# First expert layer with the high and low parts of its moving operand in one matmul, three arms of widths, and part of the weights' low parts on GpSimd

## The chip, the cores and the metric

The kernel runs on one core of one Trainium2 chip. The metric is the device time of one execution in microseconds (us). The engines are TensorE (PE in the rows, PEld for its weight loads), VectorE (DVE), ScalarE (ACT), GpSimd (POOL) and SyncE (SP, which issues most DMAs).

## What is computed

Three layers in a row, all in fp32: a sparse attention (8 global keys and a local window of 96), a mixture of 8 experts in which each token goes to one expert, and a second mixture in which each token goes through 4 experts, weighted.

```python
idx = np.argmax(logits, axis=1)                 # one of 8 experts for each of 1536 tokens
for e in range(8):                              # D = 512, F = 1024
    h = np.maximum(x[idx == e] @ w1[e], 0.0)
    out[idx == e] = gate_w[idx == e, None] * (h @ w2[e])
...
for e in range(4):
    h = np.maximum(x @ v1[e], 0.0)
    out += p[:, e:e + 1] * (h @ v2[e])
```

The change is in the first mixture, the loop over 8 experts. The router of the reference, worked out on its inputs, gives the experts 171, 247, 155, 177, 135, 215, 231 and 205 tokens.

## The kernel before, in words

fp32 products are made out of fp32r matmuls: every operand is cut into a high part (a copy rounded to fp32r) and a low part (operand minus high part), and a product is the sum of three matmuls, high x high, low x high and high x low.

**The loop of the first mixture** has 64 stages, `st = 8 * e + i`. Each uses one quarter of a weight matrix, a [128, 1024] block (512 KB). Stages 0 to 3 of an expert make the hidden layer (lines 892 to 894): two blocks f of 128 hidden units, each a sum over c = 0..3 of three matmuls, with 128 weight columns loaded for each matmul and the expert's token columns moving. Stages 4 to 7 make the output (907 to 909) in four PSUM tiles `yp[d]`, in the same way. So an expert takes 8 stages of 24 matmuls. The tokens of an expert stand in 256 columns; `each_width` branches on TensorE at run time (line 833, one branch in each stage) between 256 and 232 moving columns, by a flag that `offsets` computes from the counts. Expert 0 always takes 256 columns.

**Behind the matmuls.** `relu3` makes the hidden layer's high part on ScalarE (line 779) and its low part on VectorE (780), both out of PSUM. `flip_x` transposes the next expert's tokens on TensorE (857, four transposes) in stages 4 and 5 and cuts them with `split3` (775, 776). At the end of an expert `split3` cuts the four `yp[d]` into `x2h` and `x2l`, the input of the second mixture, at a column offset that is read at run time. The three hidden tiles rotate in the PSUM pool `ps_h`.

**The weights** run ahead. SyncE loads a block into one of 4 `raw` buffers (line 85). `split_to(st + 7)` puts the high part of block st + 6 on ScalarE (123), behind the `relu3` of stage st, and one stage later `split_low` puts its low part on VectorE (93). The load of block i + 5 is issued when the low part of block i is done. High and low parts lie in a ring of 14 tiles, seven blocks.

**Each engine works through its own queue in the order in which the program is written** (`manual_schedule`); across engines it waits on semaphores. The order within a stage is the order of the source.

**Around it.** `records` writes 12 indirect DMAs from GpSimd (821) after stage 20. In the last expert, after stages 61 and 62, GpSimd and ScalarE begin the second mixture's weights: `w_t13` (170, 171), `w_op` (ScalarE 181, GpSimd 182) and `w_t24` (174, 175). Then the last `split3` follows, and the second mixture starts with the matmuls of line 1023 (on `x2h`) and 1024 (on `x2l`), d by d. In the second mixture GpSimd makes low parts of weight blocks of [128, 1024] too (line 162).

## Time and profile before

| what | value |
|---|---|
| median of 3 runs | 794.27 us (794.21 to 795.54) |
| the profiled execution | 795.5 us, of which the span of the profile is 793.6 us |
| TensorE busy | 780.2 us (98% of the span), weight loads 717.6 us |
| VectorE, ScalarE, GpSimd busy | 537.7, 355.0 and 262.2 us |
| granted TensorE clock, mean over the span | 0.996 of full speed |

The span runs from the first to the last recorded instruction of the execution; 1.9 us of the execution lie outside it. Matmuls are pipelined and their ends are modelled, so that a matmul's own duration is longer than the distance to the next one; what a matmul costs in a stream is read from the starts.

### The profile page before, as it was taken

Reading aid. Unit: us, or ns where it says so; the run is one execution under the profiler, and the core shown is the slowest. Engines: PE = TensorE matmul, PEld = TensorE weight load, DVE = VectorE, ACT = ScalarE, POOL = GpSimd, SP = SyncE. Lnnn points to the kernel's source line nnn. Section 1 sums busy time; section 2 is a strip of 40 time slices with the busy share of each in tenths; the row PEclk is TensorE's granted clock in tenths of the full one; section 3 lists DMA queues with packets and bytes.
Section 4 is the critical chain, followed back from the end, with each engine's and each line's share of the span. In section 5 each row is a group of like instructions: output and inputs, shape, how many; then the busy total and the mean of one; then the engine's idle time right before and its main releaser. Section 6 shows DMA issues by size and latency. Waiting matters only on the chain.

```text
span 793.6 us, 14813 instructions
## 1 busy us (share of the span) xinstructions
PE 780.2 (98%) x5706; PEld 717.6 (90%) x5706; DVE 537.7 (68%) x1305; ACT 355.0 (45%) x728; POOL 262.2 (33%) x240
## 2 busy tenths in 40 slices
PE   9999999999999999999999999999999999999995
PEld 5889899999999989999899999999899999989995
DVE  7888675866666546556766766766777766676674
ACT  7899476755555544442242232332233233223221
POOL 2026560260000431451361351362163145136222
PEclk9999999999999999999999999999999999999998
DMA  7986375666665410010000100010001001000111
GB/s 223 327 287 221 119 232 201 217 210 231 217 221 201 149 54 27 28 53 27 28 27 27 54 27 27 27 54 27 27 27 55 28 27 54 1 1 1 54 54 57
DMA packets 32314, 77.97 MB, mean 98 GB/s; under 512 B 3865, under 2 KB 10281, under 8 KB 32225
## 3 DMA queue, kind: packets, MB, share of 16 engines
q1 hardware_dynamic: 29792, 70.36, 26.6%
q0 software_dynamic: 2416, 6.39, 2.3%
q8 instruction: 58, 0.95, 0.5%
q14 instruction: 32, 0.25, 0.1%
q10 hardware_dynamic: 16, 0.02, 0.0%
HBM read 66.22 MB, written 10.53 MB: 97 GB/s over the span
## 4 chain that ended last, share of the span: by engine, by line
PE 84%; DVE 8%; ACT 3%; DMA 1%; issue 1%; POOL 1%; POOLq 0%; SPq 0%; DVEq 0%; ACTq 0%
PE h L1024 10%; PE h L1023 10%; PE h L1025 10%; PE z L1117 9%; PE z L1120 9%; PE z L1119 9%; PE h L892 4%; PE h L893 4%; PE h L894 4%; PE y L909 4%; PE y L907 4%; PE y L908 4%; DVE sh L1074 2%; PE s L501 2%; PE at L528 1%; PE o L542 1%
## 5 line engine op out<-in xcount | busy, mean ns | idle before, releaser
L993 DVE SCALAR_TENSOR_TENSOR xall<-z,rsb,xall 128x256 f32<-128x256 f32 x313 | 135.2, 478 | 35.2 <-PE z L1120 34.6
L1024 PE MATMUL h<-x2l,wh 128*128 128x512 f32 (+1 forms) x400 | 152.8, 382 | 0.0
L1023 PE MATMUL h<-x2h,wh 128*128 128x512 f32 (+1 forms) x400 | 152.8, 382 | 0.0
L1025 PE MATMUL h<-x2h,wl 128*128 128x512 f32 (+1 forms) x400 | 152.2, 381 | 0.0
L1117 PE MATMUL z<-wt,sh 128*128 128x256 f32 x384 | 109.4, 285 | 0.8 <-ACT sh L1082 0.3
L1120 PE MATMUL z<-wt,sl 128*128 128x256 f32 x384 | 108.9, 284 | 0.0
L1119 PE MATMUL z<-wt,sh 128*128 128x256 f32 x384 | 108.6, 283 | 0.0
L1045 POOL TENSOR_TENSOR bl<-h,bh 128x512 fp32r<-128x512 f32 (+1 forms) x25 | 31.9, 1275 | 189.0 <-PE z L1120 164.5
L1060 ACT ACTIVATE ah<-h 128x512 fp32r<-128x512 f32 (+1 forms) x50 | 29.1, 582 | 140.6 <-PE h L1025 140.6
L1025 PEld LDWEIGHTS h<-x2h,wl 128*128 128x128 f32 x400 | 75.3, 188 | 14.7
L1023 PEld LDWEIGHTS h<-x2h,wh 128*128 128x128 f32 x400 | 75.4, 188 | 13.2
L1024 PEld LDWEIGHTS h<-x2l,wh 128*128 128x128 f32 x400 | 75.4, 188 | 12.9 <-issue 0.2
L1117 PEld LDWEIGHTS z<-wt,sh 128*128 128x128 f32 x384 | 73.5, 191 | 3.2 <-DVE xall L993 1.8
L1033 ACT ACTIVATE h<-h 128x512 f32<-128x512 f32 (+1 forms) x50 | 28.7, 573 | 103.4 <-PE h L1025 103.4
L93 DVE TENSOR_TENSOR wl<-raw,wh 128x1024 fp32r<-128x1024 f32 x62 | 74.5, 1222 | 0.0
L1119 PEld LDWEIGHTS z<-wt,sh 128*128 128x128 f32 x384 | 73.6, 192 | 0.8
L1120 PEld LDWEIGHTS z<-wt,sl 128*128 128x128 f32 x384 | 73.5, 192 | 0.3 <-DVE sl L1083 0.3
L907 PE MATMUL y<-hh,wh 128*128 128x232 f32 (+1 forms) x256 | 71.8, 280 | 0.0
L909 PE MATMUL y<-hh,wl 128*128 128x232 f32 (+1 forms) x256 | 70.6, 276 | 0.0
L908 PE MATMUL y<-hl,wh 128*128 128x232 f32 (+1 forms) x256 | 70.6, 276 | 0.0
L182 POOL TENSOR_TENSOR wt<-raw,wt 128x512 fp32r<-128x512 f32 x40 | 51.5, 1299 | 57.6 <-ACT wt L181 50.4
L1039 DVE SCALAR_TENSOR_TENSOR ss<-h,h 128x256 f32<-128x256 f32 (+1 forms) x50 | 20.5, 410 | 68.9 <-ACT h L1033 68.9
(210 smaller groups left out, 1999.6 us busy)
## 6 DMA issues: line engine op xcount, KB each, us to landing
raw<-in_moe_w_dram SPq DMA_DIRECT2D x96, 512.0 KB
xs<-zt SPq DMA_DIRECT2D x4, 1024.0 KB
xr<-xs SPq DMA_DIRECT2D x14, 256.0 KB
v<-in_v_dram SPq DMA_DIRECT2D x12, 256.0 KB
k<-in_k_dram SPq DMA_DIRECT2D x11, 256.0 KB
q<-in_q_dram SPq DMA_DIRECT2D x11, 256.0 KB
vwin<-in_v_dram SPq DMA_DIRECT2D x10, 192.0 KB
xe<-xs SPq DMA_DIRECT2D x2, 256.0 KB
```

Source lines behind the costliest of these rows:

```text
L93: eng.tensor_tensor(lo, r, hi.bitcast(F32), ALU.subtract)
L182: nc.gpsimd.tensor_tensor(t[:, 1], src, t[:, 0].bitcast(F32), ALU.subtract)
L907: nc.tensor.matmul(y_, wh[:, f, ws], a_, start=kf == 0, stop=False, skip_group_check=True)
L908: nc.tensor.matmul(y_, wh[:, f, ws], b_, start=False, stop=False, skip_group_check=True)
L909: nc.tensor.matmul(y_, wl[:, f, ws], a_, start=False, stop=kf == KF - 1, skip_group_check=True)
L993: nc.vector.scalar_tensor_tensor(a_, src[:, i], w_, a_, ALU.mult, ALU.add)
L1023: nc.tensor.matmul(pt, wh[:, d, ws], x2h[:, d, cs], start=d == 0, stop=False)
L1024: nc.tensor.matmul(pt, wh[:, d, ws], x2l[:, d, cs], start=False, stop=False)
L1025: nc.tensor.matmul(pt, wl[:, d, ws], x2h[:, d, cs], start=False, stop=d == KD - 1)
L1117: nc.tensor.matmul(pt[:, i], hh[:, f, ts_], wh[:, f, :], start=(o_ < 3 or pt is not prods[o_][3]) and i == f == 0, stop=False, skip_group_ ...
L1119: nc.tensor.matmul(pt[:, i], hh[:, f, ts_], wl[:, f, :], start=False, stop=False, skip_group_check=True)
L1120: nc.tensor.matmul(pt[:, i], hl[:, f, ts_], wh[:, f, :], start=False, stop=f == 1, skip_group_check=True)
```

## The change

Four things. The moving operand's high and low parts lie side by side (`xhl`, `hhl`, `x0`), and one matmul of twice the width multiplies both by the weights' high part into two halves of one PSUM tile; a second matmul adds the weights' low part times the operand's high part to the first half. So there are two matmuls where there were three, over the same number of columns. Whoever reads such a tile has to add the halves: `h_sum` does it on VectorE for the hidden layer (into `hs` in SBUF, one reduction for each f), `h_high` and `h_low` then work from `hs`, and `y_low` does it for the output, in two VectorE instructions for each half of d, moved to stages 0 and 1 of the next expert. PSUM holds four tiles of one f each (`hp`, which `flip_x` and `offsets` now use too) and `yp` in four banks. There are three arms, 184, 232 and 256 columns, and the branch is taken for each f. From stage 8 on the weights' low parts are made on GpSimd in the first 6 stages of an expert (experts 1 to 4) or the first 4 (experts 5 to 7), and on VectorE in the others. The 12 indirect DMAs of `records` move to stages 42 to 53, one in each, and the clearing of `x2l` by two stages.

```diff
-WIDTHS = 232, 256
+WIDTHS = 184, 232, 256
...
-    def split_to(n):
+    def split_to(n, eng=nc.vector):
-        split_low()
+        split_low(eng)
...
-        xh0, xl0 = (ring.tile([P, 1024], F32R, tag="w", name="x0").rearrange("p (k n) -> p k n", k=KD) for _ in range(2))
+        x0 = [ring.tile([P, 1024], F32R, tag="w", name="x0").rearrange("p (k a n) -> p k a n", k=2, a=2) for _ in range(2)]
         for c in range(KD):
-            nc.scalar.copy(xh0[:, c, :], xy[c])
-            nc.vector.tensor_tensor(xl0[:, c, :], xy[c], xh0[:, c, :].bitcast(F32), ALU.subtract)
+            xc = x0[c // 2][:, c % 2]
+            nc.scalar.copy(xc[:, 0, :], xy[c])
+            nc.vector.tensor_tensor(xc[:, 1, :], xy[c], xc[:, 0, :].bitcast(F32), ALU.subtract)
...
-        ps_h = mo.enter_context(tc.tile_pool(name="ps_h", bufs=3, space=PSUM))
...
-        def relu3(pt, hi, lo):
-            nc.scalar.activation(hi, pt, AF.Relu)
-            nc.vector.scalar_tensor_tensor(lo, pt, 0.0, hi.bitcast(F32), ALU.max, ALU.subtract)
...
+            ps_1 = m1.enter_context(tc.tile_pool(name="ps_1", bufs=1, space=PSUM))
...
-                pt = ps_t.tile([P, NE], F32, tag="t", name="t")
+                pt = next(hp)[:, 0, 0:NE]
...
+                nc.vector.scalar_tensor_tensor(arm, cnt[:, 0:NE], float(WIDTHS[1]), over, ALU.is_gt, ALU.add)
...
                 for t_ in range(T):
                     nc.gpsimd.indirect_dma_start(recv[t_], bass.IndirectOffsetOnAxis(ap=ri[:, t_:t_ + 1].bitcast(U32), axis=0),
                                                  rsrc[:, t_, :], None, bounds_check=NT - 1, oob_is_err=False)
+                    yield
...
                     with tc.If(wide > 0) as over:
-                        yield WIDTHS[1]
+                        with tc.If(wide > 1) as full:
+                            yield WIDTHS[2]
+                        with full.Else():
+                            yield WIDTHS[1]
                     with over.Else():
                         yield WIDTHS[0]
...
-            xh = mp1.tile([P, KD, CAP], F32R, name="xh")
-            xl = mp1.tile([P, KD, CAP], F32R, name="xl")
-            hh = mp1.tile([P, KF, CAP], F32R, name="hh")
-            hl = mp1.tile([P, KF, CAP], F32R, name="hl")
+            xhl = mp1.tile([P, KD, 2, CAP], F32R, name="xhl")
+            hhl = mp1.tile([P, KF, 2, CAP], F32R, name="hhl")
+            hs = mp1.tile([P, 2, 2, CAP], F32, name="hs")
+            late = []
 
             def flip_x(e, s_):
-                if e == 0 and s_:
-                    pt = next(hp).rearrange("p f (a n) -> p (f a) n", n=P)
-                else:
-                    pt = ps_t.tile([P, KD, P], F32, tag="t", name="t")
+                pt = next(hp).rearrange("p a (b n) -> p (a b) n", n=P)
                 x_ = xr.pop((e, s_))
                 for c in range(KD):
                     nc.tensor.transpose(pt[:, c, :], x_[:, c * P:(c + 1) * P], ident)
-                split3(pt, xh[:, :, s_ * P:(s_ + 1) * P], xl[:, :, s_ * P:(s_ + 1) * P])
+                split3(pt, xhl[:, :, 0, s_ * P:(s_ + 1) * P], xhl[:, :, 1, s_ * P:(s_ + 1) * P])
+
+            def h_sum(pt, f):
+                nc.vector.tensor_reduce(hs[:, f // 2 % 2, f % 2, :], pt.rearrange("p a n -> p n a"), AX.X, ALU.add)
+
+            def h_high(i):
+                nc.scalar.activation(hhl[:, 2 * i:2 * i + 2, 0, :], hs[:, i % 2], AF.Relu)
+                late.append(i)
+
+            def h_low():
+                while late:
+                    i = late.pop(0)
+                    hi, lo = (hhl[:, 2 * i:2 * i + 2, a] for a in range(2))
+                    nc.vector.scalar_tensor_tensor(lo, hs[:, i % 2], 0.0, hi.bitcast(F32), ALU.max, ALU.subtract)
+
+            ends = []
+
+            def y_low(j):
+                if ends:
+                    d, o_ = ends.pop(0)
+                    hi, lo = (a[:, d:d + 2, bass.ds(o_, CAP)] for a in (x2h, x2l))
+                    nc.vector.tensor_tensor(hs[:, j], yp[:, d:d + 2, 0, :], hi.bitcast(F32), ALU.subtract)
+                    nc.vector.tensor_tensor(lo, yp[:, d:d + 2, 1, :], hs[:, j], ALU.add)
+
+            def low_on(st):
+                return nc.gpsimd if st >= 8 and st % 8 < (6 if st < 40 else 4) else nc.vector
...
+                if st == 4:
                     nc.gpsimd.memset(x2l.bitcast(F32), 0.0)
                 if 2 <= st < 2 + T:
                     square(mp1, st - 2)
                 if st == 3 or 2 + T <= st:
                     next(parts, None)
                 if st == 8 + T:
-                    records(sorted_[1])
+                    sorted_[3] = records(sorted_[1])
+                if st >= 42:
+                    next(sorted_[3], None)
...
-            hp = cycle([ps_h.tile([P, 2, CAP], F32, tag="h", name="h") for _ in range(3)])
-            yp = [ps_y.tile([P, CAP], F32, tag=f"y{d}", name="y") for d in range(KD)]
+            hp = cycle([ps_1.tile([P, 2, CAP], F32, tag=f"h{j}", name="h") for j in range(4)])
+            yp = ps_y.tile([P, KD, 2, CAP], F32, name="y")
             wide = None
             for e in range(NE):
-                xa, xb = (xh, xl) if e else (xh0, xl0)
                 for i in range(4):
                     st = 8 * e + i
                     wh, wl = use(st)
-                    pt = next(hp)
-                    for w_ in each_width(e, wide):
-                        for f in range(2):
-                            ws = slice(f * P, (f + 1) * P)
+                    for f in range(2):
+                        pt = next(hp)
+                        ws = slice(f * P, (f + 1) * P)
+                        for w_ in each_width(e, wide):
                             for c in range(KD):
-                                o_, a_, b_ = pt[:, f, 0:w_], xa[:, c, 0:w_], xb[:, c, 0:w_]
-                                nc.tensor.matmul(o_, wh[:, c, ws], a_, start=c == 0, stop=False)
-                                nc.tensor.matmul(o_, wh[:, c, ws], b_, start=False, stop=False)
-                                nc.tensor.matmul(o_, wl[:, c, ws], a_, start=False, stop=c == KD - 1)
-                    relu3(pt, hh[:, 2 * i:2 * i + 2, :], hl[:, 2 * i:2 * i + 2, :])
-                    split_to(min(st + PRE, W0 + 2))
+                                a_ = (xhl[:, c] if e else x0[c // 2][:, c % 2])[:, :, 0:w_]
+                                nc.tensor.matmul(pt[:, :, 0:w_], wh[:, c, ws], a_, start=c == 0, stop=False)
+                                nc.tensor.matmul(pt[:, 0, 0:w_], wl[:, c, ws], a_[:, 0], start=False, stop=c == KD - 1)
+                        h_sum(pt, 2 * i + f)
+                    h_low()
+                    h_high(i)
+                    if i < 2:
+                        y_low(1 - i)
+                    split_to(min(st + PRE, W0 + 2), low_on(st))
                     side(st)
                 for i in range(4):
                     st = 8 * e + 4 + i
                     wh, wl = use(st)
-                    for w_ in each_width(e, wide):
-                        for f in range(2):
-                            kf = 2 * i + f
+                    for f in range(2):
+                        kf = 2 * i + f
+                        for w_ in each_width(e, wide):
                             for d in range(KD):
                                 ws = slice(d * P, (d + 1) * P)
-                                y_, a_, b_ = yp[d][:, 0:w_], hh[:, kf, 0:w_], hl[:, kf, 0:w_]
-                                nc.tensor.matmul(y_, wh[:, f, ws], a_, start=kf == 0, stop=False, skip_group_check=True)
-                                nc.tensor.matmul(y_, wh[:, f, ws], b_, start=False, stop=False, skip_group_check=True)
-                                nc.tensor.matmul(y_, wl[:, f, ws], a_, start=False, stop=kf == KF - 1, skip_group_check=True)
+                                a_ = hhl[:, kf, :, 0:w_]
+                                nc.tensor.matmul(yp[:, d, :, 0:w_], wh[:, f, ws], a_, start=kf == 0, stop=False, skip_group_check=True)
+                                nc.tensor.matmul(yp[:, d, 0, 0:w_], wl[:, f, ws], a_[:, 0], start=False, stop=kf == KF - 1, skip_group_check=True)
+                    h_low()
                     if e + 1 < NE and i < 2:
                         flip_x(e + 1, i)
                     if e + 1 < NE and i == 2:
                         ahead = wider(e + 1)
                     if i == 2 and e + 2 < NE:
                         load_x(e + 2)
-                    split_to(min(st + PRE, W0 + 2))
+                    split_to(min(st + PRE, W0 + 2), low_on(st))
                     side(st)
...
+                for d in range(0, KD, 2):
+                    nc.scalar.copy(x2h[:, d:d + 2, bass.ds(o_, CAP)], yp[:, d:d + 2, 0, :])
+                    ends.append((d, o_))
+                if e == NE - 1:
+                    for j in range(2):
+                        y_low(j)
...
-                for d in range(KD):
-                    split3(yp[d], x2h[:, d, bass.ds(o_, CAP)], x2l[:, d, bass.ds(o_, CAP)])
...
+            ps_h = m2.enter_context(tc.tile_pool(name="ps_h", bufs=3, space=PSUM))
```

## Rows read from the trace of the kernel before

**Rows 1.** The page: GB/s moved by DMA, in 40 equal slices of the span.

```profile
GB/s 223 327 287 221 119 232 201 217 210 231 217 221 201 149 54 27 28 53 27 28 27 27 54 27 27 27 54 27 27 27 55 28 27 54 1 1 1 54 54 57
```

**Rows 2.** Windows: start:end, length, busy time (and instructions) of PE, PEclk, DMA share, GB/s.

```profile
111.01:134.67 23.66, 23.66 (x203) 1.00 0.60 205
...
157.48:179.79 22.31, 22.31 (x203) 1.00 0.66 209
```

**Rows 3.** Windows, one expert: length, busy PE, PEld, DVE, ACT, POOL, PEclk, DMA.

```profile
188.20:210.50 22.30, 22.30 (x202) 22.30 (x202) 15.00 (x20) 13.59 (x22) 0.00 (x0) 1.00 0.62 213
```

**Rows 4.** Timeline of PE: start us, length us, engine, line, out<-in, shape, count.

```profile
143.62 0.27 PE L892 MATMUL h<-xh,wh 128*128 128x232 f32 x1
...
146.29 0.28 PE L892 MATMUL h<-xh,wh 128*128 128x232 f32 x1
...
280.03 0.39 PE L1025 MATMUL h<-x2h,wl 128*128 128x512 f32 x1
...
282.75 0.39 PE L1025 MATMUL h<-x2h,wl 128*128 128x512 f32 x1
```

**Rows 5.** Groups by form, 90 to 275 us: matmuls of line 892 by width.

```profile
L892 PE MATMUL h<-xh,wh 128*128 128x232 f32 x192 | 52.6, 274 | 0.0
...
L892 PE MATMUL h<-xh,wh 128*128 128x256 f32 x32 | 9.0, 281 | 0.0
```

**Rows 6.** Groups by form: count | busy us, mean ns | idle before.

```profile
L93 DVE TENSOR_TENSOR wl<-raw,wh 128x1024 fp32r<-128x1024 f32 x62 | 74.5, 1222 | 0.0
...
L530 DVE COPY ats<-at 128x512 f32<-128x512 f32 x10 | 6.9, 690 | 2.2 <-PE at L528 2.2
...
L287 DVE TENSOR_REDUCE l<-lh 128x8 f32<-128x64 f32 x12 | 3.2, 264 | 0.0
...
L288 DVE TENSOR_REDUCE sm<-l 128x1 f32<-128x8 f32 x12 | 1.9, 161 | 0.4
...
L814 DVE TENSOR_REDUCE r__1868<-tmp 128x12 f32<-128x96 f32 x1 | 0.3, 253 | 0.0
...
L821 POOL DMA_INDIRECT rec<-rsrc,ri x12 | 16.2, 1354 | 41.7 <-DVE hl L780 38.4 <-issue 3.4
```

**Rows 7.** Timeline of DVE: starts that follow each other without a wait.

```profile
173.07 0.69 DVE L780 SCALAR_TENSOR_TENSOR hl<-h,hh 128x512 fp32r<-128x512 f32 x1 [1.81 <-issue]
173.67 1.22 DVE L93 TENSOR_TENSOR wl<-raw,wh 128x1024 fp32r<-128x1024 f32 x1
174.81 0.68 DVE L780 SCALAR_TENSOR_TENSOR hl<-h,hh 128x512 fp32r<-128x512 f32 x1
```

**Rows 8.** Timeline of DVE and POOL, second mixture.

```profile
386.18 2.41 POOL L162 TENSOR_TENSOR wl<-raw,wh 128x1024 fp32r<-128x1024 f32 x1
...
387.20 1.94 DVE L1050 TENSOR_TENSOR sl<-ss,sh 128x512 fp32r<-128x512 f32 x1
388.55 1.75 POOL L170 TENSOR_TENSOR t<-raw 128x512 f32<-128x512 f32 x1
...
390.38 1.29 POOL L171 TENSOR_TENSOR raw<-raw 128x512 f32<-128x512 f32 x1
```

**Rows 9.** One line's durations, ns min/median/max.

```profile
L1062 DVE SCALAR_TENSOR_TENSOR al<-h,ah x50: 413/681/683, 286.2 to 779.6; 128x512 fp32r<-128x512 f32 x46, 128x256 fp32r<-128x256 f32 x4
```

**Rows 10.** Timeline of the passage to the second mixture, POOL, ACT and PE.

```profile
269.59 1.58 POOL L171 TENSOR_TENSOR raw<-raw 128x512 f32<-128x512 f32 x1 [1.79 <-ACT wt L181]
...
274.94 1.16 ACT L181 ACTIVATE wt<-raw 128x512 fp32r<-128x512 f32 x2 [3.11 <-POOL raw L174]
...
276.00 1.22 ACT L775 CAST x2h<-y 128x256 f32 x4
...
276.59 0.41 PE L1023 MATMUL h<-x2h,wh 128*128 128x512 f32 x1
...
276.96 0.47 PE L1024 MATMUL h<-x2l,wh 128*128 128x512 f32 x1
```

**Rows 11.** One line's durations, ns min/median/max: TensorE's branches.

```profile
L833 PEldq COMPARE_BRANCH  x64: 65/208/342, 117.8 to 271.9; - x64
```

More of the change, by code (lines that the diff above doesn't have):

```diff
@@ L784, in tile_attention_moe_moe @@
             xp = m1.enter_context(tc.tile_pool(name="xp", bufs=4))
+            ps_1 = m1.enter_context(tc.tile_pool(name="ps_1", bufs=1, space=PSUM))
             ps_y = m1.enter_context(tc.tile_pool(name="ps_y", bufs=1, space=PSUM))
             nc.gpsimd.memset(x2h.bitcast(F32), 0.0)
-            ps_t = m1.enter_context(tc.tile_pool(name="ps_t", bufs=1, space=PSUM))
             rsrc = mp1.tile([P, T, 8], F32, name="rsrc")
             def offsets():
-                pt = ps_t.tile([P, NE], F32, tag="t", name="t")
+                pt = next(hp)[:, 0, 0:NE]
                 nc.tensor.matmul(pt, ones, cum[:, T, :], start=True, stop=True)
                 cnt = mp1.tile([P, NE + 1], F32, name="cnt")
-                over = mp1.tile([P, NE], I32, name="over")
+                over = mp1.tile([P, NE], F32, name="over")
+                arm = mp1.tile([P, NE], I32, name="arm")
                 off = mp1.tile([P, NE], F32, name="off")
@@ L805, in offsets @@
                 nc.gpsimd.tensor_tensor(off, off, ebase, ALU.subtract)
-                return off, over
+                return off, arm
             def offsets2(off):
@@ L822, in records @@
                                                  rsrc[:, t_, :], None, bounds_check=NT - 1, oob_is_err=False)
+                    yield
                 nc.gpsimd.dma_start(out=rsb, in_=rec.rearrange("(t p) c -> p t c", p=P))
             def wider(e):
-                return nc.values_load(sorted_[2][0:1, e:e + 1], engines=(mybir.EngineType.PE,), min_val=0, max_val=1)
+                return nc.values_load(sorted_[2][0:1, e:e + 1], engines=(mybir.EngineType.PE,), min_val=0, max_val=2)
             def each_width(e, wide):
```

## The prediction, made before the changed kernel was run

> **What bounds it now.** I read the page first, then the windows by expert, then the timeline of each engine in one expert, then the port between two engines in the second mixture, and last the passage between the mixtures. In the windows the reader is to see that PE is busy for the whole of each stretch, at full granted clock (2.4 GHz), and that an expert with 232 columns takes 22.31 us, one with 256 23.66 us [rows 2]. In the same kind of stretch VectorE is busy 15.0 of 22.3 us, ScalarE 13.6, GpSimd 0 [rows 3]. So in this layer PE's stream alone sets the pace, and the change can gain only what it takes out of that stream, and lose what the other engines can't follow.
>
> **What a matmul costs.** Starts are read, not durations. 24 matmuls of 232 columns lie between 143.62 and 146.29 us, 111.3 ns each; 12 of 512 columns between 280.03 and 282.75, 226.7 ns each [rows 4]. At 2.4 GHz 512 columns stream in 213.3 ns, which leaves 13.3 ns for the matmul itself; 232 would then be 110.0, and are 111.3. An expert has 8 x 24 = 192 matmuls: at 232 columns they make 21.4 us, and 0.9 of the 22.31 us are the transposes. For 256 columns the 23.66 us give (23.66 - 0.9) / 192 = 118.5 ns.
>
> **The new pair.** One matmul of 2w and one of w columns replace three of w; every expert has 64 such sets.
> - 256: 226.7 + 118.5 = 345.2 against 355.5 ns: 0.7 us an expert.
> - 232: 464 columns are 193.3 + 13.3 = 206.6, the short one 111.3: 317.9 against 333.9 ns: 1.0 us.
> - 184: the long one, 368 columns, is 166.6 ns. The short one streams in 76.7 + 13.3 = 90.0 ns, but the next weights must be loaded behind it, 128 columns as everywhere. The trace shows no fp32r matmul closer to the next than 111.3 ns. Bounds 90.0 and 111.3; I take 111.3, since the 232 columns already lie above their line. Set: 277.9 ns, 56.0 less than before: 3.6 us, so 18.7 us an expert with its transposes.
>
> Which experts are narrow follows from the reference's counts, 171, 247, 155, 177, 135, 215, 231 and 205: 256 for experts 0 and 1, 184 for 2, 3 and 4, 232 for 5, 6 and 7. The trace agrees as far as it can: of experts 1 to 7 six run with 232 columns and one with 256 [rows 5] (32 matmuls of a line are one expert). Stream gain: 2 x 0.7 + 3 x 1.0 + 3 x 3.6 = 15.2 us; with the short matmul at 90.0 ns 64 x 21.3 ns = 1.4 us more for each narrow expert, 4.1 in all. The first matmul of expert 0 now waits for a low part too, one subtraction later, but the fourth c still sets that stage: 0.1 us.
>
> **VectorE.** Instructions that follow each other start 0.60 us apart at 512 elements and 1.14 at 1024 [rows 7]. For an expert from the second on: `h_sum` 8 x 0.60 = 4.8 (a reduction of 512 elements out of PSUM), `h_low` 4 x 0.60 = 2.4, `y_low` 4 x 0.60 = 2.4, flips 1.2, weights 2 x 1.14 = 2.3: 13.1 us (15.4 in experts 5 to 7). That is hidden behind 18.7 us, by itself. For the reduction the lower bound is the PSUM copy of 512 elements, 690 ns [rows 6], or 0.60 from start to start. It reads with a stride, though (the two halves alternate), and the only strided reduction (line 287) takes 264 ns for 64 elements, where 96 contiguous ones (814) take 253 and 8 (288) 161 [rows 6]: some (264 - 152) / 64 = 1.75 ns an element over 152 fixed, against (253 - 152) / 96 = 1.05. At 1.75 the reduction is 152 + 896 = 1048 ns, 0.36 more. I take 0.60, because the copy is like it in size and memory, and keep the other as a rival.
>
> **GpSimd and the port.** A low part of 1024 elements is 2.41 us there [rows 8]; six are 14.5 us of a narrow expert's 18.7, so it keeps up. But it doesn't run beside VectorE freely. At 386.18 us GpSimd starts such a subtraction; VectorE's line 1050, 512 elements with both inputs in SBUF, takes 1.94 us from 387.20, past GpSimd's end at 388.59, where line 93 does twice as many in 1.22 [rows 6, 8]; and GpSimd's next takes 1.75 instead of 1.29. They take turns, instruction by instruction. Instructions of VectorE with an input in PSUM don't wait: line 1062 never exceeds 683 ns [rows 9]. The Trainium skill (GPSIMD Engine Reference, Specifications) says the same, that GpSimd shares its SBUF interface with VectorE and collides with instructions of two SBUF inputs; by the engines' separate queues alone the sum below would be 4.8 us better, and the trace agrees with the page.
>
> Now `relu3` read PSUM, but `h_low` reads `hs` and `hhl`, both SBUF, and so do the weights' low parts. The port's own sum in a narrow expert is 14.5 + 2.4 + 2.3 = 19.2 us, above 18.7. VectorE, moreover, waits in its queue with `h_sum` behind `h_low`: 0 to 2.41 us each time; at the mean, 1.2 us for six such instructions, its queue is 13.1 + 7.2 = 20.3 us. (Bounds: 18.7, where PE still leads, and 13.1 + 14.5 = 27.6.) Four PSUM tiles let PE run some 3 us ahead and no more, so a narrow expert takes 20.3: 1.6 us lost, 4.8 for three. Experts 1 (23 us) and 5 to 7 (21.3 us; only four low parts on GpSimd, and VectorE at 15.4 plus four waits) cover it. The records' 12 x 1.35 us [rows 6] go into experts 5 and 6 beside 9.6 us of low parts; nothing waits for them before the second mixture. Weights: 8 x 512 KB and 512 KB of tokens in 20.3 us are 232 GB/s, a rate that the slices of this layer show already, and one slice has 327 [rows 1].
>
> **The passage to the second mixture.** ScalarE's two copies of line 181, released by GpSimd, end at 276.10, just as the last copies of `yp` are due (276.00); PE stops 0.14 us between 276.59 and 276.96 [rows 10]. Afterwards, counted from the start of expert 7 (end at 20.4 us): stages 56 to 59 put four low parts on GpSimd. The last needs its high part, which ScalarE makes behind `h_high` of stage 58. PE ends that stage at 7.6; with VectorE some 3 us late, `h_high` ends at 11 and the high part at 12, so GpSimd is free at 14.4. Lines 170 and 171, two of 182 and 174 come next, 5 x 1.29 = 6.4, then ScalarE's 1.16: 22.0, and 24.3 if the last low part on VectorE (1.14) and two `h_low` take the port between. So the copies of `yp` begin 1.6 to 3.9 us after the last matmul, and `x2l` is ready a copy (0.5) and two subtractions (1.2) later. PE loses 3.1 to 5.4 us there, less 0.14. With ScalarE free in time it would be 1.3. I take 4.2.
>
> **Sum.** 15.2 - 0.1 - 4.8 - 4.2 = 6.1 us. The profiled execution took 795.5 us, 1.9 of them outside the span: 789.4. The median of the runs lies 1.2 below that execution: **788.2 us**. 0.2% of 794.27 is 1.6 us, about what a measurement of this kernel can tell from no change.
>
> **Rivals.**
> 1. The strided reduction takes 1048 ns. Eight of them make 2.9 us more VectorE time in an expert; where VectorE sets the pace (experts 2 to 4) PE waits for it: 3 x 2.9 = 8.6, so 796.8 us, slower. In experts 5 to 7 the 2.9 us are still covered. It decides from 6.1 / 24 = 0.25 us more per reduction, 0.94 us, on. For it speaks line 287 [rows 6], against it that the row is 64 elements from SBUF. The Trainium skill (Advanced Engine Details and Errata, PSUM Cachelines) states lines of two fp32 values in PSUM and asks for pairs to be contiguous; by that rule this rival is the likelier. No row shows a strided read of PSUM.
> 2. The port costs nothing: `h_low` falls between GpSimd's instructions, VectorE is never late, and the passage costs 1.3. 15.2 - 0.1 - 1.2 = 13.9: 780.4 us. Against it: six of eight stages have GpSimd at work.
> 3. As 2, and the short matmul at 90 ns: 4.1 more, 776.3 us. (With VectorE late it would save next to nothing.)
> 4. The stream itself doesn't shorten: a matmul over two separate stretches costs more, or PE's branches, a median of 208 ns for 24 matmuls now [rows 11], show with two or three for each 8. The narrow arms then stay at three loads' time, and only the losses remain: 794.3 + 9, 803 us. Against it: branches leave no gap in today's starts.
>
> **Chances.** Forecast 0.47 (own range 785 to 793); rival 1 0.20 (791 to 799); rival 2 0.18; rival 3 0.05; rival 4 0.10. Leaving out rival 3, most of rival 4 and a rim gives 778.5 to 798. Faster: 0.45 + 0.02 + 0.18 + 0.05 = 0.70; within: 0.02 + 0.10 = 0.12; slower: 0.08 + 0.10 = 0.18.
>
> **What would show it.** Starts of long and short matmuls at 184: 167 and 111 ns (90: rival 3). The reduction's mean, 690 or 1048 ns. `h_low` with a minimum near 0.69 and a maximum above 2 us, with GpSimd's subtraction ending just before; if its maximum stays near 0.7, rival 2. Experts 2 to 4 near 20 us, with PE waiting for VectorE; experts 5 to 7 near 21.3, 0 and 1 near 23. A stop of PE of 3 to 5 us before line 1023's successor. Wrong it would be above all by a second wait that I put on covered experts, or by a PE clock that falls in the stop.

## The result and the profile after

The changed kernel takes 805.93 us (median of 4 runs, 804.36 to 808.56) where the kernel before took 794.75 beside it: ratio 1.0143, 95% interval 1.0114 to 1.0172. It is 1.4% slower; 788.2 was forecast, with 798 as the upper end. Its profiled execution took 805.72 us, its span is 804.0. Ratios are of runs in the chip's fast state; of all runs below one, 811.41 us of arms_only, is counted as slow and left out of its ratio.

The windows by expert (start:end, length, busy PE, PEld, DVE, ACT, POOL with counts, PEclk, DMA share, GB/s) answer to [rows 2, 3]:

```profile
95.80:119.46 23.66, 23.66 (x139) 20.62 (x138) 20.74 (x34) 15.10 (x27) 16.25 (x15) 1.00 0.58 197
119.46:142.81 23.35, 23.35 (x139) 20.58 (x137) 21.33 (x24) 18.13 (x32) 15.97 (x7) 1.00 0.63 220
142.81:169.06 26.25, 21.36 (x139) 20.34 (x137) 23.24 (x33) 13.50 (x19) 15.25 (x6) 0.93 0.49 165
169.06:189.70 20.64, 19.41 (x139) 18.82 (x137) 19.87 (x21) 12.39 (x16) 15.19 (x6) 1.00 0.66 232
189.70:210.34 20.64, 19.40 (x139) 18.80 (x137) 20.23 (x21) 12.39 (x16) 15.54 (x6) 1.00 0.66 231
210.34:231.94 21.60, 21.60 (x138) 20.09 (x137) 21.00 (x24) 12.51 (x16) 15.98 (x9) 1.00 0.65 225
231.94:254.59 22.65, 22.03 (x139) 20.10 (x137) 20.95 (x23) 12.40 (x16) 20.52 (x12) 1.00 0.64 213
254.59:280.87 26.28, 22.63 (x130) 20.46 (x128) 22.39 (x18) 9.50 (x13) 17.28 (x9) 0.94 0.49 159
```

From expert 2 on, but for expert 5, PE no longer fills the stretches, while VectorE is busy for 85 to 98% of them. Experts 0, 1 and 5 gained a little and 3 and 4 1.7 us each, but expert 2, as narrow as 3 and 4, takes 26.25, and expert 7 26.05 to its last `y` matmul at 280.63 (21.33 before). The first 24 matmuls of the second mixture take 11.9 us from there, where they took 5.6. At the 24th the kernel is 10.4 us late (292.50 against 282.07), and after it nothing changes. Three stops of TensorE (stretches in which it has no matmul to run) make most of this, and three slow stretches behind them. Windows, columns as above:

```profile
149.60:153.10 3.50, 0.41 (x4) 0.22 (x2) 1.84 (x5) 1.57 (x3) 2.34 (x1) 0.97 0.07 25
153.10:157.00 3.90, 3.90 (x17) 3.90 (x18) 3.80 (x7) 1.58 (x2) 1.85 (x1) 0.59 0.47 129
...
264.90:268.70 3.80, 0.20 (x2) 0.00 (x0) 3.64 (x3) 0.00 (x0) 1.70 (x1) 1.00 0.71 227
268.70:272.50 3.80, 3.75 (x13) 3.44 (x14) 3.69 (x6) 2.06 (x3) 0.81 (x1) 0.55 0.14 53
280.90:285.90 5.00, 0.60 (x3) 0.29 (x2) 1.54 (x3) 2.64 (x5) 4.92 (x5) 1.00 0.09 26
285.90:289.50 3.60, 3.60 (x9) 2.85 (x10) 1.13 (x2) 0.00 (x0) 1.30 (x2) 0.53 0.37 133
```

Behind each stop the granted clock falls to its lower level, 1.2 GHz, for most of some 4 us: 3.9 x 0.41 + 3.8 x 0.45 + 3.6 x 0.47 = 5.0 us lost.

**Expert 2.** Timeline of DVE, then one row of ACT, then PE at the stop:

```profile
146.70 1.29 DVE L860 TENSOR_REDUCE hs<-h 128x256 f32<-128x512 f32 x2 [0.15 <-issue]
...
148.62 0.69 DVE L879 TENSOR_TENSOR x2l<-y,hs 128x512 f32 x1
151.23 0.25 DVE L756 TENSOR_REDUCE g<-ge 128x12 f32<-128x96 f32 x1 [1.92 <-ACT ge L755]
...
152.19 1.27 DVE L860 TENSOR_REDUCE hs<-h 128x256 f32<-128x512 f32 x2
...
149.62 1.28 ACT L755 ACT_TABLE_LOAD   x1
...
149.40 0.25 PE L919 MATMUL h<-xhl,wl 128*128 128x184 f32 x1
149.48 0.36 PE L918 MATMUL h<-xhl,wh 128*128 128x368 f32 x1
149.68 0.25 PE L919 MATMUL h<-xhl,wl 128*128 128x184 f32 x1
153.01 0.65 PE L918 MATMUL h<-xhl,wh 128*128 128x368 f32 x1 [3.09 <-DVE hs L860]
```

The PSUM tiles are full until `h_sum` (860) empties one, and `h_sum` stands on VectorE behind the gate's parts (744 to 764; the gate works out the tokens' weights in small steps, called by `side`). The part at 151.23 us waits for ScalarE's Exp (755), which has an `h_high` (0.63 us), a high part of the weights (1.04) and the load of ScalarE's function table (1.28) ahead of it. The PE rows also show a pair: 0.08 us from the start of a short matmul to the long one, 0.20 from the long to the short.

**Expert 7.** Timeline of POOL, DVE and PE:

```profile
258.41 1.11 POOL L822 DMA_DIRECT2D rsb<-rec  x1 [4.30 <-issue]
259.54 7.06 POOL L93 TENSOR_TENSOR wl<-raw,wh 128x1024 fp32r<-128x1024 f32 x3
...
260.70 6.45 DVE L870 SCALAR_TENSOR_TENSOR hhl<-hs,hhl 128x512 fp32r<-128x512 f32 x1
...
267.91 0.69 DVE L879 TENSOR_TENSOR x2l<-y,hs 128x512 f32 x1
...
268.75 0.57 PE L936 MATMUL y<-hhl,wh 128*128 128x464 f32 x1 [3.65 <-DVE x2l L879]
```

The last DMA of `records` (822) stood 4.30 us at the head of GpSimd's queue, and three low parts came ready behind it. They run without a break, and one `h_low`, 0.68 us at its shortest, ends at 267.15, 0.55 us behind the third. TensorE waits for the `x2l` behind it.

**The passage.** Timeline of POOL, ACT and PE, to compare with [rows 10]:

```profile
280.89 1.25 POOL L174 TENSOR_TENSOR raw<-raw,t 128x512 f32<-128x512 f32 x1
...
282.18 1.15 ACT L181 ACTIVATE wt<-raw 128x512 fp32r<-128x512 f32 x2 [4.05 <-POOL raw L174]
283.24 1.05 ACT L961 CAST x2h<-y 128x512 f32 x2
...
283.86 0.49 PE L1057 MATMUL h<-x2h,wh 128*128 128x512 f32 x1 [2.95 <-ACT x2h L961]
285.80 0.65 PE L1058 MATMUL h<-x2l,wh 128*128 128x512 f32 x1 [1.45 <-DVE x2l L879]
286.24 0.63 PE L1059 MATMUL h<-x2h,wl 128*128 128x512 f32 x1
```

The copies of `yp` stand on ScalarE behind two of line 181 that wait for GpSimd. TensorE stops 3.2 and 1.9 us; after that a matmul of 512 columns takes 0.43 us from start to start.

### The profile page after: what moved, and what is told of

The parts are those of the page before. It is cut to its first block, busy times and chain, and to the rows that moved or that the text cites. A ratio compares the mean times of both kernels' runs of the same rounds, so it can differ in the third digit from the quotient of the medians.

```text
span 804.0 us, 14058 instructions
## 1 busy us (share of the span) xinstructions
PE 774.9 (96%) x5194; PEld 698.1 (87%) x5194; DVE 590.6 (73%) x1334; ACT 353.8 (44%) x712; POOL 355.6 (44%) x276
## 3 DMA queue, kind: packets, MB, share of 16 engines
q1 hardware_dynamic: 29792, 70.36, 25.8%
## 4 chain that ended last, share of the span: by engine, by line
PE 55%; DVE 7%; ACT 1%; issue 0%; POOLq 0%; POOL 0%; DVEq 0%
PE h L1058 10%; PE h L1059 10%; PE h L1057 10%; PE z L1151 9%; PE z L1154 9%; PE z L1153 9%; DVE sh L1108 2%; DVE al L1096 1%; DVE xall L1027 1%; DVE sl L1109 1%; DVE ss L1095 1%; ACT sh L1116 1%; DVE sl L1117 1%; DVE ss L1107 1%; DVE ss L1112 1%; ACT ah L1094 1%
## 5 line engine op out<-in xcount | busy, mean ns | idle before, releaser
L93 POOL TENSOR_TENSOR wl<-raw,wh 128x1024 fp32r<-128x1024 f32 x36 | 90.7, 2532 | 42.1 <-ACT wh L123 38.1
L936 PE MATMUL y<-hhl,wh 128*128 128x464 f32 (+2 forms) x256 | 84.8, 385 | 8.5 <-DVE x2l L879 5.0
L918 PE MATMUL h<-xhl,wh 128*128 128x368 f32 (+2 forms) x224 | 71.4, 378 | 3.1 <-DVE hs L860 3.1
L123 ACT ACTIVATE wh<-raw 128x1024 fp32r<-128x1024 f32 x61 | 64.2, 1053 | 17.7 <-DMA raw<-in_moe_w_dram 17.2
```

What stands on the lines that cost most here:

```text
L93: eng.tensor_tensor(lo, r, hi.bitcast(F32), ALU.subtract)
L123: nc.scalar.activation(hi, r, AF.Copy)
L918: nc.tensor.matmul(pt[:, :, 0:w_], wh[:, c, ws], a_, start=c == 0, stop=False)
L936: nc.tensor.matmul(yp[:, d, :, 0:w_], wh[:, f, ws], a_, start=kf == 0, stop=False, skip_group_check=True)
```

## The experiments

The theory after the result: the loss is those three stops and the clock behind them, each with a cause of its own. Rivals: the merged pairs or the narrow arms don't give what they should, or VectorE is too slow by its added work, whoever else is at the port (what GpSimd and VectorE share on the way to SBUF). Lengths are in us, from the first matmul of an expert to the next expert's; "24" is the time from the last `y` matmul to the 24th matmul after it. Before is 794.47 to 795.54 us beside the runs.

| run | median us | ratio (95% interval) | e2 | e3 | e4 | e5 | e6 | e7 | 24 |
|---|---|---|---|---|---|---|---|---|---|
| before | 794.75 | | 22.3 | 22.3 | 22.3 | 22.3 | 22.3 | 21.3 | 5.6 |
| after | 805.93 | 1.0143 (1.0114 to 1.0172) | 26.2 | 20.6 | 20.6 | 21.6 | 22.7 | 26.0 | 11.9 |
| arms_only | 805.03 | 1.0100 (1.0068 to 1.0133) | 22.2 | 32.2 | 22.9 | 22.3 | 22.6 | 21.3 | 6.3 |
| two_arms | 808.31 | 1.0158 (1.0140 to 1.0175) | 26.6 | 21.6 | 21.6 | 21.6 | 22.3 | 27.6 | 11.9 |
| low_vec | 800.74 | 1.0068 (1.0051 to 1.0085) | 24.3 | 20.0 | 20.6 | 22.1 | 21.8 | 23.1 | 12.8 |
| gate_late | 805.75 | 1.0146 (1.0125 to 1.0168) | 21.4 | 25.9 | 20.6 | 21.6 | 22.2 | 26.0 | 12.4 |
| rsb_late | 801.94 | 1.0091 (1.0075 to 1.0108) | 26.4 | 20.0 | 21.6 | 21.6 | 22.7 | 20.9 | 14.0 |
| last_vec | 802.64 | 1.0099 (1.0076 to 1.0122) | 26.5 | 22.2 | 21.2 | 21.6 | 22.6 | 21.7 | 12.7 |
| copy_first | 803.84 | 1.0101 (1.0080 to 1.0122) | 26.2 | 21.4 | 20.6 | 21.6 | 22.7 | 25.8 | 8.1 |
| mend | 798.03 | 1.0022 (1.0009 to 1.0036) | 21.6 | 24.1 | 21.6 | 23.4 | 22.7 | 21.0 | 9.7 |
| pool_y | 804.26 | 1.0121 (1.0106 to 1.0137) | 24.1 | 21.1 | 20.7 | 22.7 | 23.1 | 24.8 | 12.9 |
| best_y | 809.76 | 1.0190 (1.0175 to 1.0205) | 25.8 | 23.4 | 25.9 | 23.4 | 22.2 | 23.0 | 9.7 |
| vec_mend | 794.80 | 0.9999 (0.9988 to 1.0010) | 20.7 | 21.5 | 21.2 | 21.8 | 21.6 | 21.7 | 9.7 |
| vec_pass | 794.36 | 0.9991 (0.9982 to 0.9999) | 20.7 | 21.5 | 21.2 | 23.3 | 21.6 | 21.7 | 8.4 |

**arms_only**, on the kernel before:

```diff
-WIDTHS = 232, 256
+WIDTHS = 184, 232, 256
...
+                        with tc.If(wide > 1) as full:
...
```

> The kernel before with the third arm of 184 rows alone: three matmuls a set, one after the other, no merging, no reduction, no low parts on GpSimd. In the changed kernel a short matmul of 184 columns is followed by the next after 83 ns. If the columns alone set the pace, three take 250 to 270 ns instead of 334, an expert of 184 rows 17 to 18.2 us instead of 22.3, the time falls by 12 to 15 us: 780 to 783. Rival (loading the next weights sets it, and the 111.3 ns of 232 columns is already that floor, as the prediction took it): no gain, 793 to 796. Of theory and rival on the loss: whichever holds, VectorE, which has 15 us of work in an expert here and no stop, shows none of the three stops.

The rival holds: three matmuls of 184 columns start 112 ns apart, as those of 232 do, so the arm alone gives nothing. In the profiled execution the time is worse than forecast by one event, 9.9 of 11.5 us. Timeline of PE in expert 3, and two windows:

```profile
171.04 0.28 PE L898 MATMUL h<-xl,wh 128*128 128x184 f32 x1
171.15 0.27 PE L899 MATMUL h<-xh,wl 128*128 128x184 f32 x1
172.94 0.35 PE L897 MATMUL h<-xh,wh 128*128 128x184 f32 x1 [1.52 <-issue]
...
165.90:170.00 4.10, 4.10 (x39) 4.10 (x38) 1.62 (x5) 1.79 (x4) 3.19 (x4) 1.00 0.93 281
...
174.00:190.00 16.00, 16.00 (x78) 16.00 (x78) 5.38 (x7) 4.53 (x7) 1.11 (x1) 0.50 0.36 109
```

A stop of 1.8 us, at a stage's branch and with no engine to wait for, is followed by 16 us at 1.2 GHz, 8 us lost. What made it stop is not known. Nor is that event all: the two runs whose mean clock is that of the kernel before (0.998 and 0.996) took 798.69 and 801.04 us, 4 to 7 us more than it, and no trace of them shows where. The other four took 804.29 to 811.41.

**two_arms**, on the changed kernel, as all that follow:

```diff
-WIDTHS = 184, 232, 256
+WIDTHS = 232, 232, 256
```

> The changed kernel with the narrow arm at 232 columns too: merged pairs, same branches, no 184. Theory (experts 2 to 4 are bound by VectorE at 20 to 20.6 us, so the 184 columns are worth 1.0 us each and no more, and the three stops have other causes): experts 3 and 4 take 21.7 us, the stop in expert 2 stays at 2 to 3.5 us, the one in 7 and the one at the passage stay: 807 us (805 to 809). Rival (it is the 184 columns that let TensorE outrun VectorE into the stop of expert 2): that stop goes with its half clock, 802 to 804.

As the theory has it: 184 columns are worth 0.9 us in each of experts 3 and 4 (21.57 against 20.64), and the stop of expert 2 is 2.55 us without them.

**low_vec**

```diff
-                return nc.gpsimd if st >= 8 and st % 8 < (6 if st < 40 else 4) else nc.vector
+                return nc.vector
```

> The changed kernel with all low parts of the weights on VectorE, none on GpSimd. Theory (the 1.9 us of h_low, against 0.68 at its shortest, and most of VectorE's lateness is waiting for the port, not work): h_low takes 0.7 us everywhere, VectorE's own work in an expert is 8 x 1.14 + 8 x 0.6 + 12 x 0.6 + 1.2 = 22.3 us at most, so the experts of 184 and 232 rows all take 21.6 to 22.3 us, the stops in expert 7 go, the one in expert 2 stays with the gate's parts: 802 us (800 to 805). Rival (VectorE's 20 us in an expert are work): six more low parts of 1.14 us make an expert 26 to 27 us, 825 to 840.

The theory holds: no expert takes 26 us. Experts 3 and 4 are faster than expected, expert 7 is slower (23.1): GpSimd's line 170 falls beside an `h_low` there (1.72 us at 267.80), and TensorE stops 1.41 us behind it. Groups of lines 870 and 860 of the changed kernel (its window of expert 4 stands above), and then line 870 and the window of expert 4 of this run:

```profile
L870 DVE SCALAR_TENSOR_TENSOR hhl<-hs,hhl 128x512 fp32r<-128x512 f32 x32 | 59.6, 1880 | 0.0
L860 DVE TENSOR_REDUCE hs<-h 128x256 f32<-128x512 f32 x64 | 41.7, 686 | 8.3 <-PE h L919 6.0 <-PE h L789 0.3 <-issue 0.2
```

```profile
L870 DVE SCALAR_TENSOR_TENSOR hhl<-hs,hhl 128x512 fp32r<-128x512 f32 x32 | 24.0, 751 | 0.0
...
187.36:207.99 20.63, 19.64 (x139) 18.84 (x137) 20.23 (x27) 12.02 (x16) 0.00 (x0) 1.00 0.69 232
```

VectorE is busy 20.23 us in expert 4 with all eight low parts and 20.23 with two. What GpSimd takes off, 36 low parts of 1.14 us or 41 us in all experts, comes back as waits for the port: 59.6 - 24.0 = 35.6 us in `h_low` alone.

**gate_late**

```diff
-                if st == 3 or 2 + T <= st:
+                if st == 3 or 20 <= st:
```

> The gate's last four parts in stages 20 to 23 (second half of expert 2, where TensorE fills no fresh PSUM tile) instead of 14 to 17. Theory (the stop of 3.33 us at 149.7 comes from VectorE's queue standing on those parts, with only four PSUM tiles ahead): the stop and the half clock behind it go, expert 2 falls from 26.25 to 21 to 22.5 us, and the time by 4 to 5: 802 us (800 to 803). Rival (the parts cost VectorE's queue the same anywhere): the stop is found again in expert 2 or 3, 806 us.

The rival holds: the stop (3.52 us) is at the start of expert 3. There VectorE isn't idle ahead of it, it is late by the parts themselves, two of them lengthened beside GpSimd:

```profile
162.29 1.53 DVE L745 TENSOR_SCALAR g<-g 128x12 f32<-128x12 f32 x1
...
167.25 2.45 DVE L758 TENSOR_TENSOR ge<-ge,oh 128x96 f32<-128x96 f32 x1
169.63 1.21 DVE L93 TENSOR_TENSOR wl<-raw,wh 128x1024 fp32r<-128x1024 f32 x1
...
171.99 1.29 DVE L860 TENSOR_REDUCE hs<-h 128x256 f32<-128x512 f32 x2 [0.19 <-issue]
```

So it isn't the stage that decides but that VectorE has no room in a narrow expert for four parts in a row. Nor does the port decide it: low_vec, with no low part on GpSimd, keeps a stop of 2.70 us in expert 2. With one part in each of four experts (mend, vec_mend) the stop is gone.

**rsb_late and last_vec**

```diff
                     yield
+                for _ in range(6):
+                    yield
                 nc.gpsimd.dma_start(out=rsb, in_=rec.rearrange("(t p) c -> p t c", p=P))
```

```diff
-                return nc.gpsimd if st >= 8 and st % 8 < (6 if st < 40 else 4) else nc.vector
+                return nc.gpsimd if 8 <= st < 56 and st % 8 < (6 if st < 40 else 4) else nc.vector
```

> GpSimd's last DMA of the records, which stood 4.3 us at the head of its queue before three low parts, is issued six stages later. Theory (the low parts piled up behind it, and only a pile of ready instructions on GpSimd keeps VectorE off the port for their whole length): GpSimd's low parts of expert 7 run one by one with VectorE's in between, h_low there stays under 3 us, expert 7 takes 22 to 23 us and the passage 2 us less: 799 us (797 to 802). Rival (GpSimd holds the port whenever two of its instructions are ready, and pile or not they are ready in expert 7): h_low of 5 us or more is seen in expert 7 again, 804 to 807.

> Low parts of the last expert back on VectorE, the rest as in the changed kernel. Theory (the loss is three stops of TensorE, and the one in expert 7 comes from GpSimd's low parts that hold the shared port back to back for 7.06 us): h_low in expert 7 stays under 3 us, the stop of 3.9 us at 264.8 goes, expert 7 takes 21.5 to 22.5 us instead of 26.3, GpSimd is free for line 170 as soon as its raw weights are there, and the passage gets 2 to 4 us shorter: 799 us (796 to 801). Rival (VectorE is late because of its added work, whoever else is at the port): four parts of 1.2 us more on VectorE keep expert 7 at 26 us or above, 805 to 810.

Both take the stop out of expert 7, rsb_late without moving any work off GpSimd. Its timeline of POOL and DVE there:

```profile
257.00 2.39 POOL L93 TENSOR_TENSOR wl<-raw,wh 128x1024 fp32r<-128x1024 f32 x1 [1.96 <-PE h L921]
260.74 2.41 POOL L93 TENSOR_TENSOR wl<-raw,wh 128x1024 fp32r<-128x1024 f32 x1 [1.35 <-PE h L920]
...
261.62 2.07 DVE L872 SCALAR_TENSOR_TENSOR hhl<-hs,hhl 128x512 fp32r<-128x512 f32 x1
```

Here the low parts hold `h_low` up 1.4 to 2.1 us; behind the DMA, 5.7 to 6.0 in all four runs that have the pile of three low parts behind it (after, gate_late, copy_first, two_arms). The pile alone, rsb_late's theory, doesn't do it. In each of experts 1 to 4 of the changed kernel three low parts run in a row with no DMA ahead, and VectorE gets a turn after each. Timeline of POOL and DVE in expert 4:

```profile
202.14 8.01 POOL L93 TENSOR_TENSOR wl<-raw,wh 128x1024 fp32r<-128x1024 f32 x3 [1.40 <-PE h L856]
...
202.60 5.31 DVE L870 SCALAR_TENSOR_TENSOR hhl<-hs,hhl 128x512 fp32r<-128x512 f32 x2
```

Nor is a DMA right ahead enough by itself: in rsb_late lines 170 and 171 follow the same DMA (270.57) without a break, and an `h_low` (2.49 us at 271.09) gets its turn behind the first. What the two together do to the port stays open. And the passage doesn't get shorter (14.0 and 12.7 us), so that 4.0 of 5.1 us and 3.3 of 4.4 reach the time; there my theory of last_vec was wrong: GpSimd was free, but line 170 waited for its load until 272.24.

**copy_first**

```diff
-                        elif i == 2:
-                            w_op(0, 2)
-                            load_to(W0 + 3 + RAW)
-                            w_op(0, 3)
...
                     for j in range(2):
                         y_low(j)
+                    w_op(0, 2)
+                    load_to(W0 + 3 + RAW)
+                    w_op(0, 3)
```

> The changed kernel with ScalarE's two copies of x2h (and VectorE's x2l behind them) issued ahead of the third and fourth operand of the second mixture, which ScalarE can only copy once GpSimd has made them. Theory (TensorE's stop at the passage is ScalarE's queue standing on GpSimd): of the 3.22 and 1.94 us in which it stops there 2 to 3 are left, too short for the clock to fall, and the 3.5 us at half clock behind it go: 801 us (799.5 to 803). Rival (GpSimd's chain is late in any order, and what is not waited for before line 1057 is waited for at the operands' first use): a new stop before line 1151, 804 to 807.

The stops fall to 1.00 and 1.94 us, the clock stays at 2.4 GHz there, and the passage gives back 3.8 us in the profiled execution, of which 2.1 are seen in the median (3.3 by the ratio); the time is just above the range. That 2 to 3 us are too short for the clock to fall is no rule, though: in low_vec a stop of 2.70 us is followed by 4.6 us at 1.2 GHz, in arms_only one of 1.79 by 16 us.

**Four versions that put cures together.** All have copy_first's edit and one gate part in each of four experts, but for pool_y, which moves the low parts alone.

```diff
-                if st == 3 or 2 + T <= st:
+                if st in (3, 14, 22, 30, 38):           # mend, with rsb_late and two_arms
+                if st in (3, 14, 20, 28, 36):           # best_y, with rsb_late and pool_y; vec_mend, with low_vec
...
+                return nc.gpsimd if 8 <= st < 56 and st % 8 > 4 else nc.vector     # pool_y
```

> Four cures in one kernel: the records' last DMA six stages later, x2h's copies ahead of the third and fourth operand, the gate's four parts in the second halves of experts 1, 2, 3 and 4 (one each) instead of in four stages in a row, and 232 columns in place of 184, so that VectorE's 20 us have 1.7 us to spare in each expert. Theory (three stops and the half clock behind them are the whole loss): no stop of TensorE above 1.5 us before the passage, where 2 to 2.5 are left; the last y matmul at 272 to 273.5 us against 276.5 in the kernel before: 792.5 us (790.5 to 795). Rival (VectorE is late on the whole, and stops come back elsewhere): 797 to 802.

> The changed kernel with GpSimd's low parts moved from the first six (four) stages of an expert to its last three, and none in the last expert; the other five on VectorE. Theory (the port is lost to h_low, x2l and the gate, which read SBUF twice and stand in stages 0 to 4; in stages 5 to 7 VectorE reads PSUM): h_low averages under 1.0 us, VectorE's work in an expert of 184 rows is some 22 - 3 x 1.14 = 18.6 us, experts 3 and 4 take 18.8 to 19.6 us (TensorE's own 18.8), expert 7 about 21.5, and the stop of expert 2 stays: 797.5 us (795 to 800). Rival (VectorE loses to GpSimd wherever both work): experts 3 and 4 stay at 20.3 us or above, 800 to 803.

> As the run with the low parts in the last three stages, with the three cures: the records' last DMA six stages later, x2h's copies ahead of the third and fourth operand, the gate's four parts at stages 14, 20, 28 and 36. Theory: experts 2 to 4 take 19.5 to 20 us, 5 and 6 21.6, 7 21.0, so the last y matmul comes at 266 to 269 us against 276.5 in the kernel before, and 24 matmuls of the second mixture take 8.1 us from there against 5.6: 788 us (785 to 791), faster than the kernel before. Rival (what is taken off one stage of VectorE's queue comes back in another, as in the run with four cures): 794 to 798.

> As the run with all low parts on VectorE, with x2h's copies ahead of the third and fourth operand and the gate's parts at stages 14, 20, 28 and 36. Theory: the passage gives back 4 to 5 us of that run's time and the stop of expert 2 with its half clock 1.5 to 3 (VectorE has no room in experts 2 to 4, so each gate part costs there 1 us): 794.5 us (792.5 to 797). Rival (without room on VectorE the stops come back one for one): 797 to 800.

In mend the stops of experts 2 and 7 are gone and the passage takes 9.7 us, but with GpSimd at the port experts 3 and 5 lose 2.5 and 1.8 us against expert 4, with a stop of 1.5 in each, and the last `y` matmul comes at 277.4: its rival holds. The theories of pool_y and best_y were wrong, and both times lie above their rivals' too. `h_low` is 715 ns in pool_y, as forecast, but the three low parts become ready together, when TensorE frees their tiles in the ring. Timeline of POOL, DVE and PE in expert 2 of best_y:

```profile
160.49 7.80 POOL L93 TENSOR_TENSOR wl<-raw,wh 128x1024 fp32r<-128x1024 f32 x3 [14.26 <-PE y L938]
...
163.99 2.09 DVE L751 TENSOR_TENSOR ge<-l,g 128x96 f32<-128x96 f32 x1
...
166.40 2.00 DVE L753 TENSOR_TENSOR ge<-ge,g 128x96 f32<-128x96 f32 x1
168.32 0.68 DVE L776 TENSOR_TENSOR xhl<-h,xhl 128x512 fp32r<-128x512 f32 x1
...
169.15 0.65 PE L920 MATMUL h<-xhl,wh 128*128 128x368 f32 x1 [6.35 <-DVE xhl L776]
```

VectorE gets one turn for each low part, but lines 751 and 753 of the gate, 0.26 us by themselves, and line 749, 0.17, spend such a turn each and take 1.7 to 2.1 us; TensorE stops 6.6 us, and in expert 4 6.5 us once more. Why pool_y's experts 5 to 7 lose 1.1, 1.5 and 3.8 us was not followed further.

vec_mend, without GpSimd at the port, met its forecast: no stop above 1.5 us in the experts, the last `y` matmul at 272.2 against 276.5. The passage takes it all back (9.7 us against 5.6), with a granted clock of 0.70 of full speed behind stops of 1.1 and 1.9 us.

**vec_pass** is vec_mend with two edits at the passage:

```diff
+                    if st == W0 - 1:
+                        rounds = [[(f, d) for d in range(KD) for f in range(2)]]
...
                     ends.append((d, o_))
+                    if e == NE - 1:
+                        y_low(d // 2)
```

> As the run with all low parts on VectorE and the two cures, with two more edits at the passage: the last stage of expert 7 goes through its outputs one after the other (both inner parts of the first two, then of the last two), so that these are final 1.3 us before TensorE is through, and each copy of x2h is followed at once by its x2l instead of both copies first. Theory (the 1.09 and 1.94 us in which TensorE stops there are a chain of one copy, 0.55, the second, 0.53, and two subtractions, 1.4, behind the last matmul, and the half clock follows from them): 0.7 to 1.2 us of stop are left, no half clock, 24 matmuls of the second mixture 6.3 to 6.8 us from the last y matmul instead of 9.7: 791.5 us (790 to 793.5), faster than the kernel before. Rival (it is not the stops at the passage: the clock falls there anyway, or the matmuls wait for something else): 794 to 796.

The first edit did nothing: ScalarE's copy of the first two outputs starts at 273.81, after the last `y` matmul (273.44), so it waits for all four. The second cut one stop from 1.94 to 1.45 and moved part of it (0.81) six matmuls on; no half clock follows, and the 24 matmuls take 8.4 us where 6.3 to 6.8 were expected. An expert 5 that is 1.5 us longer in this execution hides it, so that the time is the rival's, though the clock held. vec_mend and vec_pass are within 0.2% of the kernel before.

## Why the prediction was wrong

- **Stream gain, 15.2: 13.1.** It is 0.4 and 0.3 us for 256 columns, 0.7 where 232 run free, 0.4 in expert 7 (20.94 in rsb_late), and 3.5 for 184. The last is worked out from the pairs' starts (64 x 280 ns and 0.9 us of transposes make 18.8 us); no narrow expert ran that free. A pair of 184 takes 280 ns (277.9 forecast), but as 197 + 83 and not 167 + 111; at 232 it takes 325, at 256 352, 7 more than forecast each. That the narrow arm needs the pair, arms_only shows. Rival 4 is near in time (803), but its mechanism isn't there; rival 3's short matmul (83) comes with a long one that takes back what it saves.
- **`h_sum`: 686 ns over 64 of them (line 860 above).** Rival 1 fell: every second element lies 1 KB away, and it takes no longer than the plain copy of 512 elements out of PSUM, 690 ns [rows 6]. The Trainium skill (Advanced Engine Details and Errata, PSUM Cachelines) asks that every two consecutive elements be contiguous for best throughput. For this VectorE instruction the measurement does not bear that out.
- **VectorE in a narrow expert, 20.3: 20.64** in experts 3 and 4, a loss of the kind and size that was forecast. The mean wait of an `h_low`, 1.2 us forecast, is 1.4 there (2.04 us each).
- **The step that failed first: VectorE's sum of 13.1 us "for an expert from the second on".** It left out the gate's parts. They stood in stages 14 to 17 before, too, where VectorE had 7 us to spare; with none to spare they stop TensorE. Expert 2 lost 7.5 us where 1.6 were forecast. gate_late and vec_mend show the cause: with the parts moved out of its first half expert 2 is 4.9 us shorter (21.35) and the stop comes in expert 3, and with the parts spread there is none.
- **The second: "They take turns, instruction by instruction", and with it that experts 5 to 7 cover VectorE's waits.** Elsewhere the turns came as forecast, but behind GpSimd's DMA VectorE got none during three low parts, 5.8 us, and that decided expert 7 (5.1 us, by rsb_late). Expert 6 lost 1.05; in vec_mend, without low parts on GpSimd, it takes 21.57 and loses nothing. Rival 2, that the port costs nothing, is as wrong: an `h_low` takes 1.88 us on average, 0.75 in low_vec. That moving the low parts to GpSimd spares VectorE nothing, low_vec shows too. The Trainium skill (GPSIMD Engine Reference, Specifications) names this collision between GpSimd and VectorE's instructions with two SBUF inputs. The trace agrees: 1.88 against 0.75 us.
- **The passage, 4.2 (3.1 to 5.4): 6.3.** The chain was right, and the stops (4.8 beyond a normal start) lie in the bounds. But GpSimd's low parts are not its only cause: without them (last_vec, low_vec) line 170 waits for its load, and TensorE's stops are as long (3.7 and 1.9 us in low_vec). The half clock behind the stops, 1.7, was named as what would make the prediction wrong, and was in no sum; nor was the one behind the other two stops.

Sum: 13.1 - 7.5 (expert 2) - 3.7 (experts 3 and 4) - 1.05 (6) - 5.1 (7) - 6.3 (passage) = -10.5 us; measured -10.4. The losses are differences to the lengths behind the 13.1, so that the sum closes by itself; what each is due to is shown by the runs.

## What to carry to other kernels

Before an engine is given work in a layer, count everything in its queue stage by stage, small parts with waits of their own too: what slack covered costs its full length once the slack is gone. Work moved from VectorE to GpSimd was worth nothing here, where both read SBUF at the same time. It was worse where small instructions of VectorE each spent a turn, or where GpSimd's piled up behind a DMA of its own and ran in one piece. So look at what the moved work will run beside. A stop of TensorE has a second price, the clock behind it, that belongs into the sum.

## What was not expected of the hardware

- Three subtractions of GpSimd right behind a DMA that it had issued kept VectorE out of the port for all of them, 5.8 us; without a DMA ahead VectorE got its turn after each of three (202.14 us).
- A TENSOR_SCALAR of VectorE with 12 elements and one input waits for GpSimd too: line 745 took 1.53 us in gate_late, 0.17 without GpSimd. The reciprocals and reductions next to it don't: lines 750 and 752 of best_y took 0.23 and 0.25 us while GpSimd was at work.
- TensorE's clock falls behind stops of different length and for different times: 16 us after a stop of 1.8, some 4 after 3.3 to 5, not at all after 1.5, nor after 2.25 us in last_vec (expert 3, from 178.88 us). The same 1.0 and 1.9 us at the passage were followed by a lower clock in vec_mend and not in copy_first.
